# Denominators from sums over 384 of 512 queries, weights one load earlier, norm scratch in the destination, and a new table of shifts

## The chip, the cores and the metric

The kernel runs on one core of a Trainium2 chip. The time of a run is the device time in microseconds (us) of that core, and a kernel's time is the median of its runs. The core has a tensor engine (TensorE, PE in the profile, with its weight loads as PEld), a vector engine (VectorE, DVE), an activation engine (ScalarE, ACT), GpSimd (POOL) and a queue for transfers (SyncE, SP). Each works through its own list of instructions in order and waits for the others through semaphores.

## The reference

An attention layer with a compressive memory and a feed-forward layer, in bf16, over 2048 tokens of width 1024. The 32 heads have width 32; the tokens come in four segments of 512. Cut to what is computed:

```python
def _A_ref(x, wq, wk, wv, wo, beta):          # H = 32, Dh = 32, N = 4 segments, L = 512
    phi = lambda t: where(t > 0, t + 1.0, exp(t))
    g = sigmoid(beta)                          # per head
    M, z = 0, 0
    for s in range(N):
        qs, ks, vs = q[:, :, s], k[:, :, s], v[:, :, s]
        logits = einsum('bhqd,bhkd->bhqk', qs, ks) * Dh ** -0.5 + causal_mask
        a_dot = softmax(logits) @ vs
        pq = phi(qs)
        a_mem = (pq @ M) / (pq @ z + 1e-06)
        outs.append(g * a_mem + (1.0 - g) * a_dot)
        pk = phi(ks)
        M = M + einsum('bhld,bhle->bhde', pk, vs)
        z = z + sum_l(pk)
    return concat(outs) @ wo

def reference(...):
    h = x + _A_ref(layernorm(x), wq, wk, wv, wo, beta)
    n = layernorm(h)
    return h + (silu(n @ w1) * (n @ w3)) @ w2  # w1, w3: 1024 x 3584; w2: 3584 x 1024
```

## The kernel before

**Staging.** The activations of a segment are normalised, transposed (the first segment on TensorE, later ones by a transposing DMA) and projected to q, k and v (`project`), with weights that stream in in halves of 1 MB (`wp`). Then come, for each segment and each half of the heads (16 heads, four groups of four), the attention steps of `attention`; then the output projection and the residual (`wo_stage`, L1361), the second norm (`ln`, L880), and the feed-forward layer in two blocks of 1024 tokens (`ffn_up`, L1389 to L1397, and `ffn_down`). All dense matmuls are recorded at L747 and the transposes of the start at L759; evictions from PSUM are at L770 (ACT) and L771 (DVE).

**Attention of a half.** `scores` (L1081) makes ten sets of scores. A set is four concurrent row tiles of 32 contracted elements (L1101), is followed by one exponential of 2048 columns on ACT into a buffer `et` (L1115), and by a causal mask on GpSimd for the tiles on the diagonal (L1124). Keys are taken in blocks of 128 (`kc` 0 to 3), queries before a key block are left out, so that block `kc` has 512 - 128 kc columns. `finish` (L1159) then makes the numerators (`et` against `v`) and the denominators (`et` against ones) as column tiles, four heads at once (`column`, L1187 and L1194), in four numerator columns with the denominators ahead of the last one. After them ACT and DVE copy the numerators out (`Nsb`, L1245 and L1246), DVE transposes the denominators (`T`, L1225) and takes reciprocals (L1236), and these are spread over the rows by transposes (L1257), or, in the segments 2 and 3, by a trip through a buffer in DRAM, `r_scr` (written by a load-list entry recorded at L322, read back at L1281). The retrieve from the memory is a matmul with 32x32 tiles (L1316), whose result is scaled on DVE (`R`, L1329) and added into `oT` on GpSimd or DVE (L1332); `oT` is what the output projection reads. `attention` calls the retrieve of a half in the middle of the next half's scores.

**Sums for the denominators.** A denominator is a sum over all keys. To spare TensorE a part of it, `gather` (L1131, adds at L1138) adds the exponentials of different key blocks on DVE. Before, for the queries from 256 on, all four key blocks are added: per pair of head groups six adds, four of 4x256 columns and two of 4x128. TensorE then takes per head three pieces: key block 0 for the queries below 256, the sum for those from 256 on, and key block 1 for the queries 128 to 255, which makes 256 + 256 + 128 columns. The two sum buffers of a half lie over `R0` and `R1`, which are not in use then.

**The start.** `first_half` (L961) lists the loads of the first segment: x tiles 0, 1, 2, the first half of the first wq, x tile 3, the first half of the first wk, the rest of them and wv. They go through one queue in this order. `first_tile` (L891) normalises an x tile, transposes it on TensorE in two halves, and evicts the transposes. The statistics of tile 2 wait until the first half of tile 0 has been normalised.

**What sets the order.** The kernel text declares operations with their reads and writes. A planner (`Graph.schedule`) runs a list scheduler over them with a cost for each, and writes a fixed order for every engine; semaphores are then placed from that order. An operation has a class and a sequence number, and the ready operation with the lowest pair goes first. A table `SHIFT` changes both per unit (a unit is about one group of declared operations): the first number moves the sequence, the second the class. Costs in the planner only shape the order. Between the last scores of a half and its column work no transfers are put into the queue.

**Norm scratch.** Some of the second norms (`ON_ACT`) take their statistics on ACT, by two activations whose summed output is what counts; the full-width output is written to a buffer `junk` that nothing reads.

Of the kernel before, what the change touches and what calls it, by code (L numbers as in the profile page):

```python
# [25 lines left out]
ADDED = ((1, 2, 3),) * 4  # L26
# [4 lines left out]
    0: (-18, 0), 3: (-173, 0), 4: (-182, 0), 5: (1074, 0), 6: (1041, 1), 7: (-959, -1),  # L31
    8: (-283, 1), 9: (1560, 1), 10: (-14, 0), 11: (1, 0), 12: (51, -1), 13: (-257, 0),
    14: (-1703, 0), 15: (2952, 0), 16: (-2912, 0), 18: (-87, -1), 19: (3455, 1), 20: (-401, -1),
    21: (22, 0), 22: (2924, -1), 23: (-669, 0), 24: (-328, -1), 26: (-261, -1), 27: (11, -1),
    28: (-153, 0), 29: (-317, 0), 31: (1524, -1), 32: (211, 0), 33: (-1, 0), 34: (2, 0),
    35: (-15, 0), 38: (118, 1), 39: (2057, 0), 40: (223, 0), 41: (2279, -1), 42: (914, 1),
    43: (-1135, 1), 44: (2665, 1), 45: (3218, 1), 47: (1997, 1), 48: (664, -1), 49: (1928, -1),
    50: (-2800, -1), 51: (7, 0), 52: (-1130, 0), 53: (116, 0), 54: (669, 0), 55: (1018, 0),
    56: (2, 0), 57: (-289, 1), 58: (4, 0), 59: (731, 0), 60: (-304, 0), 61: (-436, 0),
    62: (64, 1), 63: (-3, 0), 64: (-63, 0), 65: (-50, 0), 66: (-174, 0), 67: (-937, 0),  # L40
    68: (808, 0), 69: (1512, -1), 70: (28, 0), 71: (-58, 1), 72: (1441, 1), 73: (-75, 1),
    74: (2141, 0), 75: (778, 1), 76: (-752, 1), 77: (90, 1), 78: (-21, 0), 79: (151, 0),
    80: (1343, 0), 81: (-1130, 0), 83: (160, 0), 84: (687, 0), 85: (-676, 0), 86: (312, 0),
    87: (-266, 0), 88: (-263, 0), 89: (-1189, -1), 90: (-164, 0), 91: (680, 1), 92: (-1801, 0),
    93: (1499, 0), 94: (3153, 0), 95: (-261, 0), 96: (0, -1), 97: (-11, 0), 98: (2, 0),
    99: (944, 0), 100: (-54, 0), 101: (1016, 0), 102: (-842, 0), 103: (147, 0), 104: (-1191, 0),
    106: (-47, 0), 107: (121, 1), 108: (-1142, 0), 109: (-1295, -1), 111: (699, 0),
    112: (-365, -1), 113: (-594, 0), 115: (28, 0), 116: (2452, -1), 117: (-8, 0), 118: (676, 0),
    119: (54, 0), 120: (-1449, -1), 121: (235, 0), 122: (-9, -1), 123: (-13, 1), 124: (45, 0),
    125: (-1279, 1), 127: (-283, -1), 129: (555, 0), 130: (1438, -1), 132: (617, 1),  # L50
    133: (81, 0), 134: (-2285, -1), 135: (-179, 0), 136: (3199, 1), 137: (389, 0),
    138: (920, 0), 139: (146, 1), 140: (687, 1), 141: (27, 0), 142: (-619, 1), 143: (1934, 1),
    144: (-922, 0), 145: (415, -1), 146: (-312, 0), 147: (-26, 0), 148: (-870, 0),
    149: (2501, 1), 150: (1682, 0), 151: (-28, 0), 152: (609, 1), 153: (611, 0), 154: (-302, 0),
    156: (0, 1), 157: (-185, 1), 158: (391, 0), 159: (-373, 0), 160: (-610, 0), 161: (-1748, 0),
    162: (-133, 0), 163: (-4056, 1), 164: (1073, 1), 166: (-202, 0), 168: (-3204, -1),
    169: (-2075, -1), 170: (2581, -1), 171: (-39, 1), 172: (-122, 1), 173: (-18, 1),
    174: (-37, 0), 175: (34, 0), 176: (1853, 1), 177: (-140, 0), 178: (-301, 0), 179: (204, 0),
    181: (165, 0), 182: (-13, 0), 183: (-7, 0), 184: (687, -1), 185: (-271, 0), 186: (-861, 1),
    187: (-616, 1), 188: (355, -1), 189: (-1449, 1), 190: (1132, 0), 191: (114, 0),  # L60
    192: (-22, 0), 193: (-464, 0), 194: (-2, 0), 195: (294, 0), 196: (18, 0), 197: (-2089, 0),
    199: (-2443, 0), 200: (248, -1), 201: (1, 0), 203: (210, 1), 204: (-1070, 0), 206: (-70, 0),
    207: (1441, 0), 208: (525, 0), 209: (839, 0), 210: (10, 0), 211: (-262, 0), 212: (894, -1),
    213: (203, 1), 214: (-359, 1), 215: (-2, 0), 216: (696, -1), 217: (-735, 0), 218: (-51, 0),
    219: (4750, 0), 220: (-465, -1), 221: (-23, 0), 222: (-196, 1), 223: (399, 0),
    224: (-1932, 1), 225: (-192, 0), 226: (-134, 0), 227: (-1542, 1), 229: (153, 1),
    230: (-676, 1), 231: (-73, 0), 232: (618, 1), 234: (-465, 0), 235: (0, -1), 237: (222, -1),
    238: (609, 0), 239: (1282, 0), 241: (-183, 1), 242: (845, 1), 243: (811, -1),
    244: (1681, -1), 246: (6, 1), 248: (-2423, -1), 249: (11, 0), 250: (21, 0), 251: (-2902, 1),
    252: (-599, 1), 253: (927, 0), 255: (308, -1), 256: (4, -1), 257: (-382, 0), 258: (30, 0),  # L70
    259: (-35, 0), 260: (-73, -1), 261: (-386, 0), 262: (-58, 1), 263: (-1713, 0),
    264: (-165, 0), 265: (-369, 1), 266: (-12, 0), 267: (808, -1), 268: (1356, 0),
    269: (-538, 0), 270: (576, -1), 272: (27, 0), 273: (609, 0), 275: (-27, 0), 277: (0, -1),
    279: (-4, 0), 280: (-3, 0), 281: (176, 0), 282: (-28, -1), 284: (-175, -1),
    285: (-1255, -1), 286: (-196, 0), 287: (308, 0), 288: (1028, 0), 289: (-18, 0),
    290: (-217, -1), 291: (628, 0), 292: (21, 0), 293: (11, 0), 294: (1042, 0), 295: (6, 0),
    296: (150, -1), 297: (222, 0), 298: (1329, 0), 299: (-799, 0), 300: (-3, 0), 301: (303, -1),
    302: (-473, -1), 303: (2419, -1), 304: (528, 0), 305: (-99, 0), 306: (2531, -1),
    307: (-28, 0), 309: (-1338, 1), 310: (-4, 1), 311: (836, 0), 312: (-154, 0), 315: (-261, 0),
    316: (443, 0), 317: (-31, -1), 318: (-1464, -1), 319: (-220, 0), 320: (340, 0),  # L80
    321: (1268, 0), 322: (-21, -1), 323: (-2755, 1), 324: (-54, 0), 325: (1643, -1),
    326: (-57, 0), 327: (1851, 0), 328: (-2912, 0), 329: (317, 1), 330: (-690, 0),
    331: (-712, -1), 332: (-940, 0), 333: (-1099, 1), 334: (-615, 1), 335: (-16, 0),
    336: (496, 0), 337: (664, 0), 338: (-166, 0), 339: (-46, 0), 340: (-700, 0), 341: (-385, 1),
    342: (-1713, 0), 344: (51, 0), 345: (-756, -1), 346: (178, -1), 348: (803, 0),
    350: (1942, -1), 351: (169, 0), 352: (-492, 1), 354: (14, 0), 355: (-39, 0), 356: (290, 0),
    357: (99, 0), 358: (-389, 0), 359: (1761, 0), 361: (1409, 0), 362: (-58, -1), 363: (550, 1),
    364: (-95, 1), 365: (-140, 1), 366: (56, 1), 367: (-11, 1), 368: (-1627, 0),
# [519 lines left out]
class Kernel:  # L608
# [480 lines left out]
    def scores(self, s, g0, i, parts, at):  # L1089
# [38 lines left out]
        if s == 0 and not g0 and i == GATES:  # L1128
            self.gates()

    def gather(self, i, at, added):  # L1131

        pair, i = divmod(i, 5)
        S, g = self.sums[pair], 2 * pair
# [6 lines left out]
        for n, step in ((0, 1), (1, 4)):  # L1141
            todo = {0: 3 * n, 1: step, 2: 2, 3: step}
            s, done = S[:, :, n, :], None
            for kc in sorted((0,) + added, key=lambda kc: (max(todo[kc], todo[0]), kc != 0, kc == 3)):
                when = max(todo[kc], todo[0])
                if when > i:
                    break
# [363 lines left out]
```

The softmax here doesn't subtract the row's maximum and nothing guards it: scores larger than these inputs give would overflow.

## Time and profile before

| | before |
|---|---|
| time, median of 3 runs | 888.77 us (888.38 to 888.92) |
| span of the profiled run | 886.3 us, TensorE clock 1.000 |
| TensorE busy | 873.0 us, 99% of the span |
| VectorE busy | 449.2 us, 51% |
| ScalarE busy | 302.5 us, 34% |
| GpSimd busy | 178.4 us, 20% |

A line of a group of instructions reads: line of the kernel, engine, operation, output and inputs by name with their shape, number; then busy time in us and the mean of one in ns; then the idle time of the engine just before such instructions and what ended it. A line of the timeline begins with the start and the length in us, and a bracket at its end tells how long the engine was idle before and what ended that. Matmuls overlap, so the mean of one is longer than the distance between two. "ps" is PSUM.

### The profile page before, as it was taken

The page shows a single profiled execution, that of the slowest core. Times are in us where ns is not written, and L with a number is a line of the kernel's source. Part 1 is how long each engine was busy: PE and PEld are TensorE (multiplying, and loading weights), DVE is VectorE, ACT ScalarE, POOL GpSimd, SP SyncE. Part 2 cuts the span into 40 slices and gives each one's busy share as a digit, 9 for nine tenths or more (in the row PEclk, how much of TensorE's full clock was granted, in tenths as well). Part 3 has the DMA queues.
Part 4 walks back from the last instruction along what each step waited for, and adds up shares of the span by engine and source line. Part 5 has one row for each costly group of instructions (what it writes and reads, how often), then busy time and mean ns, then how long its engine had stood idle before and what let it go on. Part 6 is the DMA issues. An engine that isn't in the chain of part 4 may idle for free.

```text
span 886.3 us, 13649 instructions
## 1 busy us (share of the span) xinstructions
PE 873.0 (99%) x5732; PEld 400.5 (45%) x5821; DVE 449.2 (51%) x699; ACT 302.5 (34%) x345; POOL 178.4 (20%) x226
## 2 busy tenths in 40 slices
PE   9999999999999999999999999999999999999998
PEld 5444444444444344444444444444444444444445
DVE  6697878786665797645545301323243333341011
ACT  5878675779645555511111000101011111110000
POOL 2544443455252455303000000000000000000000
PEclk9999999999999999999999999999999999999999
DMA  7869939464862736198354410221323321301010
GB/s 238 208 185 244 227 91 267 125 156 119 217 155 74 175 83 156 53 300 258 103 156 107 120 35 30 78 65 54 83 61 88 95 72 48 90 7 41 30 54 24
DMA packets 148796, 105.75 MB, mean 119 GB/s; under 512 B 46336, under 2 KB 134400, under 8 KB 147712
## 3 DMA queue, kind: packets, MB, share of 16 engines
q1 hardware_dynamic: 148736, 104.89, 44.5%
q8 instruction: 46, 0.75, 0.4%
q14 instruction: 14, 0.11, 0.0%
HBM read 84.94 MB, written 9.44 MB: 106 GB/s over the span
## 4 chain that ended last, share of the span: by engine, by line
PE 94%; DMA 2%; DVE 2%; issue 1%; POOL 0%; ACT 0%; SPq 0%; ACTq 0%; POOLq 0%; DVEq 0%
PE ps L747 88%; PE ps L1194 3%; PE ps L1101 3%; DMA R0w<-r_scr 1%; DMA r_scr<-T 1%; DVE oT L1332 0%; SPq L1281 0%; DMA xs<-in_A_x_dram 0%; PE ps L1029 0%; DVE lnst L874 0%; ACT et L1115 0%; PE ps L1316 0%; POOL et L1124 0%; DVE hm L1397 0%; PE ps L1187 0%
## 5 line engine op out<-in xcount | busy, mean ns | idle before, releaser
L747 PE MATMUL ps<-hnT,w1b 128*128 128x512 bf16 x875 | 219.8, 379 | 2.0 <-issue 0.5
L747 PE MATMUL ps<-hnT,w3b 128*128 128x512 bf16 x879 | 217.1, 379 | 1.5 <-issue 0.5
L747 PE MATMUL ps<-w2b,hm 128*128 128x512 bf16 (+2 forms) x935 | 198.5, 366 | 0.9
L1389 ACT ACTIVATE sg<-ps 128x512 bf16<-128x512 f32 x112 | 66.8, 597 | 385.9 <-PE ps L747 385.8
L1392 DVE SCALAR_TENSOR_TENSOR t<-sg,ps 128x512 bf16<-128x512 bf16 x112 | 76.7, 685 | 183.1 <-ACT sg L1389 182.6
L1115 ACT ACTIVATE et<-ps 128x2048 bf16<-128x2048 f32 x80 | 150.0, 1874 | 45.1 <-PE ps L1101 44.7
L747 PEld LDWEIGHTS ps<-w2b,hm 128*128 128x128 bf16 x952 | 90.9, 98 | 103.0
L747 PEld LDWEIGHTS ps<-hnT,w1b 128*128 128x128 bf16 x896 | 86.2, 98 | 106.3 <-issue 6.5
L747 PEld LDWEIGHTS ps<-hnT,w3b 128*128 128x128 bf16 x896 | 86.3, 98 | 106.1 <-issue 3.6
L1124 POOL TENSOR_SCALAR_AFFINE_SELECT et<-et 128x512 bf16<-128x512 bf16 (+1 forms) x96 | 93.1, 976 | 133.0 <-ACT et L1115 132.7
L1397 DVE SCALAR_TENSOR_TENSOR hm<-t,ps 128x512 bf16<-128x512 bf16 x112 | 76.2, 685 | 40.8 <-PE ps L747 39.0
L1421 DVE TENSOR_TENSOR ob<-hr,ps 128x512 bf16<-128x512 bf16 (+2 forms) x34 | 22.2, 655 | 120.6 <-PE ps L747 120.4
L747 PE MATMUL ps<-wo,oT 128*128 128x512 bf16 x246 | 60.9, 379 | 1.1 <-issue 0.8
L747 PE MATMUL ps<-xnT,wp 128*128 128x512 bf16 (+1 forms) x345 | 59.6, 320 | 1.3 <-issue 0.8
L747 PE MATMUL ps<-hnT,wp 128*128 128x512 bf16 x249 | 59.4, 380 | 0.8 <-issue 0.6
L1138 DVE TENSOR_TENSOR sum<-sum,et 128x512 bf16<-128x512 bf16 (+1 forms) x64 | 43.6, 684 | 11.6 <-POOL et L1124 6.1
L747 PEld LDWEIGHTS ps<-xnT,wp 128*128 128x128 bf16 x352 | 28.0, 98 | 26.9 <-issue 2.8
L747 PEld LDWEIGHTS ps<-wo,oT 128*128 128x128 bf16 x256 | 23.9, 98 | 29.9 <-issue 3.3
L747 PEld LDWEIGHTS ps<-hnT,wp 128*128 128x128 bf16 x256 | 23.5, 98 | 29.7 <-issue 3.9
L1101 PE MATMUL ps<-qT,kT 32*128 32x128 bf16 (+3 forms) x512 | 31.7, 301 | 0.0
L747 PE MATMUL ps<-wp,xnT 128*128 128x512 bf16 x123 | 30.2, 379 | 0.4 <-issue 0.2
L747 PE MATMUL ps<-wp,hnT 128*128 128x512 bf16 x123 | 29.6, 380 | 0.5 <-issue 0.3
(97 smaller groups left out, 560.1 us busy)
## 6 DMA issues: line engine op xcount, KB each, us to landing
w3b<-in_B_w_dram SPq DMA_DIRECT2D x28, 512.0 KB, 4.1
w1b<-in_B_w_dram SPq DMA_DIRECT2D x28, 512.0 KB, 4.0
wp<-in_A_wv_dram SPq DMA_DIRECT2D x8, 1024.0 KB, 6.5
wp<-in_A_wq_dram SPq DMA_DIRECT2D x7, 1024.0 KB, 5.6
wp<-in_A_wk_dram SPq DMA_DIRECT2D x7, 1024.0 KB, 7.2
w2b<-in_B_w_dram SPq DMA_DIRECT2D x7, 1024.0 KB, 5.8
xs<-in_A_x_dram SPq DMA_DIRECT2D x16, 256.0 KB, 5.9
h<-in_A_x_dram SPq DMA_DIRECT2D x16, 256.0 KB, 4.0
```

The costliest lines, as they stand in the source:

```text
L747: return [e.matmul(p[0](gr), p[1], p[2], start=p[3], stop=p[4]) for p in part]
L1101: ins.append(e.matmul(self.bank(gr, j, 512 - 128 * kc, off), k[r, g0 + g, 128 * kc:128 * kc + 128], q[r, g0 + g, 128 * kc:512], start=True ...
L1115: return [e.activation(et[:, :, :], src, AF.Exp, scale=self.scale)]
L1124: self.pool_op(lambda e, v=v, pat=pat: e.affine_select(v, v, pattern=pat, compare_op=ALU.is_ge, fill=0.0, base=0, channel_multiplier=-1), ...
L1138: lambda e, gr: [e.tensor_tensor(out, x, y, op=ALU.add)], reads=[x, y],
L1194: ins.append(e.matmul(self.ps[32 * i:32 * i + 32, b * 512 + c0:b * 512 + c0 + n], lhsT(i, kc, j), rhs(i, j), start=kc == 0 and j == first, ...
L1389: self.g.op("act", act_ns(512), lambda e, gr, sg=sg: [e.activation(sg, self.bank(gr), AF.Tanh, scale=0.5)], writes=[sg], cls=0, group=gg)
L1392: e.scalar_tensor_tensor(t1, sg, 1.0, self.bank(gr), op0=ALU.add, op1=ALU.mult)], reads=[sg], writes=[t1], cls=0,
L1397: e.scalar_tensor_tensor(dst, t1, 0.5, self.bank(gr), op0=ALU.mult, op1=ALU.mult)], reads=[t1], writes=[dst], cls=0,
L1421: self.g.op("dve", dve_ns(n), lambda e, gr, hs=hs, ob=ob, n=n: [e.tensor_tensor(ob, hs, self.bank(gr, 0, n), op=ALU.add)], reads=[hs], wri ...
```

## The change

Five edits are made together.

1. The sums take in all queries but the first 128 (384 columns instead of 256). TensorE needs two pieces per head instead of three: key block 0 for the first 128 queries, and the sum for the other 384. `gather` makes seven adds per pair instead of six: for the first head group of a pair 4x384, 4x128 and 4x256 columns, for the second 4x256, 4x256, 4x128 and 4x128. This is to take work off TensorE.
2. The two sum buffers become 6144 bytes each and lie one after the other over `R0`, 2048 free bytes and the beginning of `R1`. The bytes come from `junk`: the norm's activations write their unused output into `hn`, where the normalised row is put afterwards.
3. The first half of the first wq is loaded ahead of x tile 2, so that the first projection can begin earlier.
4. The first eviction of tile 0's transposes is put on VectorE, and the statistics of tile 2 wait for it.
5. The table `SHIFT` is another one throughout, so the order on every engine changes, in the feed-forward layer less than in the attention.

The diff without the table and without the lines of the removed name `ADDED`:

```diff
-        self.junk = buf("junk", [128, 1024], BF16)
...
         self.R0 = buf("R0", [128, 2, 512], F32)
+        take(2048)
         self.R1 = buf("R1", [128, 4, 512], F32)
...
-        self.sums = [buf(f"sum{i}", [128, 4, 2, 256], BF16, self.g.base[t.name][1])
-                     for i, t in enumerate((self.R0, self.R1))]
+        self.sums = [buf(f"sum{i}", [128, 4, 2, 384], BF16, self.g.base[self.R0.name][1] + 6144 * i)
+                     for i in range(2)]
...
-        var, mean, op = self.ln_act(k, src, self.junk[:, :], cls - 1) if k in ON_ACT else self.ln_stats(k, src, cls - 1)
+        var, mean, op = self.ln_act(k, src, dst, cls - 1) if k in ON_ACT else self.ln_stats(k, src, cls - 1)
...
-            t, x, 1, (self.applied[0],) if t else ())
+            t, x, 1, (self.copied,) if t else ())
...
-            self.evac(gr, out, 512, lambda v: v[:, 0:512].rearrange("p (k n) -> p k n", k=4),
-                      cls=1, bf=True, engs=("dve", "act"))
+            o = self.evac(gr, out, 512, lambda v: v[:, 0:512].rearrange("p (k n) -> p k n", k=4),
+                          cls=1, bf=True, engs=("dve", "act") if t or b else ("dve",))
+            if t == 0 and not b:
+                self.copied = o
...
-        loads = [x[0] + (1.04,), x[1] + (0.7,), x[2] + (1.2,),
-                 (wq[:, :, 0:256], sq[:, :, 0:256], 1.54), x[3] + (0.65,),
+        loads = [x[0] + (1.04,), x[1] + (0.7,), (wq[:, :, 0:256], sq[:, :, 0:256], 1.3),
+                 x[2] + (1.0,), x[3] + (0.65,),
...
-        for n, step in ((0, 1), (1, 4)):
-            todo = {0: 3 * n, 1: step, 2: 2, 3: step}
-            s, done = S[:, :, n, :], None
-            for kc in sorted((0,) + added, key=lambda kc: (max(todo[kc], todo[0]), kc != 0, kc == 3)):
-                when = max(todo[kc], todo[0])
-                if when > i:
-                    break
-                x = at[g + n, kc][:, :, 256 - 128 * kc if kc < 2 else 0:512 - 128 * kc]
-                if done is None:
-                    done = x
-                    continue
-                if when == i:
-                    if kc == 3:
-                        add(s[:, :, 128:256], s[:, :, 128:256], x, 512)
-                    else:
-                        add(s, done, x, 1024)
-                done = s
+        for n in range(2):
+            D, s = S[:, :, n, :], [at.get((g + n, kc)) for kc in range(4)]
+            if n == 0 and i == 1:
+                add(D, s[0][:, :, 128:512], s[1], 1536)
+                add(D[:, :, 256:384], D[:, :, 256:384], s[3], 512)
+            elif n == 0 and i == 2:
+                add(D[:, :, 128:384], D[:, :, 128:384], s[2], 1024)
+            elif n == 1 and i == 3:
+                add(D[:, :, 128:384], s[0][:, :, 256:512], s[2], 1024)
+            elif n == 1 and i == 4:
+                add(D[:, :, 128:384], D[:, :, 128:384], s[1][:, :, 128:384], 1024)
+                add(D[:, :, 256:384], D[:, :, 256:384], s[3], 512)
+                add(D[:, :, 0:128], s[0][:, :, 128:256], s[1][:, :, 0:128], 512)
...
-        denom = [(0, lambda i, j: at[i, 0][:, j, 0:256], 0, 256),
-                 (1, lambda i, j: self.sums[i // 2][:, j, i % 2, :], 256, 256)] if added else numer[:1]
-        for kc in (1, 2, 3):
-            n = (128 if kc == 1 else 0) if kc in added else 512 - 128 * kc
-            if n:
-                denom.append((kc, lambda i, j, kc=kc, n=n: at[i, kc][:, j, 0:n], 128 * kc, n))
+        denom = [(0, lambda i, j: at[i, 0][:, j, 0:128], 0, 128),
+                 (1, lambda i, j: self.sums[i // 2][:, j, i % 2, :], 128, 384)]
```

The table's first entries, as an example of what it holds:

```diff
-    0: (-18, 0), 3: (-173, 0), 4: (-182, 0), 5: (1074, 0), 6: (1041, 1), 7: (-959, -1),
+    0: (2251, 0), 3: (-192, 0), 4: (703, 0), 5: (938, 0), 6: (37, 0), 7: (-2876, -1),
```

## The prediction

> **What bounds the kernel now.** I read the engine totals first, then the chain that ended last, then the groups of instructions by shape, and last the timeline around the places that the change touches.
>
> ```profile
> PE 873.0 (99%) x5732; PEld 400.5 (45%) x5821; DVE 449.2 (51%) x699; ACT 302.5 (34%) x345; POOL 178.4 (20%) x226
> PE 94%; DMA 2%; DVE 2%; issue 1%; POOL 0%; ACT 0%; SPq 0%; ACTq 0%; POOLq 0%; DVEq 0%
> ```
>
> TensorE (PE) is busy all the time and is 94% of the chain. So a microsecond of TensorE work removed is worth a microsecond, work of another engine costs nothing while TensorE has something to do, and every new hole in TensorE's stream is paid in full. From start to start of consecutive matmuls (a dense 128x512 one every 0.216 us) I find only 3.7 us of real holes in 886.3: 1.22 in the first 12 us, and 2.45 later, at 174.5 (0.33), 257.7 (0.13), 266 (0.38), 297.8 (0.92), 308.7 (0.54) and 457.5 (0.15).
>
> ```profile
> L1115 ACT ACTIVATE et<-ps 128x2048 bf16<-128x2048 f32 x80 | 150.0, 1874 | 45.1 <-PE ps L1101 44.7
> L1124 POOL TENSOR_SCALAR_AFFINE_SELECT et<-et 128x1024 bf16<-128x1024 bf16 x32 | 45.3, 1417 | 60.1 <-ACT et L1115 60.1
> L1138 DVE TENSOR_TENSOR sum<-sum,et 128x1024 bf16<-128x1024 bf16 x32 | 29.8, 933 | 9.5 <-ACT et L1115 5.3 <-POOL et L1124 4.2
> L1138 DVE TENSOR_TENSOR sum<-et,et 128x1024 bf16<-128x1024 bf16 x32 | 26.7, 838 | 4.4 <-ACT et L1115 4.4
> L1332 POOL TENSOR_TENSOR oT<-Nsb,R 128x512 bf16<-128x512 f32 x15 | 22.4, 1515 | 1.4 <-DVE R L1329 1.4
> L1138 DVE TENSOR_TENSOR sum<-sum,et 128x512 bf16<-128x512 bf16 x32 | 13.9, 435 | 2.1 <-POOL et L1124 2.0
> L1194 PE MATMUL ps<-et,ones 128*32 128x256 bf16 x128 | 8.9, 273 | 0.0
> L1194 PE MATMUL ps<-sum,ones 128*32 128x256 bf16 x128 | 8.9, 273 | 0.0
> L1194 PE MATMUL ps<-et,ones 128*32 128x128 bf16 x128 | 7.4, 219 | 0.0
> ```
>
> The price list: an exponential 1.87 us, the mask of a last tile 1.42, one product into oT 1.52, an add 0.44 to 0.93. The last three rows are the denominators; their means are latencies of overlapped matmuls, so I price them from starts:
>
> ```profile
> 93.44 0.28 PE L1194 MATMUL ps<-et,ones 128*32 128x256 bf16 x4
> 93.55 0.28 PE L1194 MATMUL ps<-sum,ones 128*32 128x256 bf16 x4
> 93.66 0.34 PE L1194 MATMUL ps<-et,ones 128*32 128x128 bf16 x8
> ...
> 94.48 0.23 PE L1194 MATMUL ps<-et,ones 128*32 128x128 bf16 x4
> 94.53 0.72 PE L1194 MATMUL ps<-et,v 128*32 128x512 bf16 x16
> ```
>
> One round of 256+256+128 columns takes 0.273 us; four rounds make the 1.09 us from 93.44 to 94.53. Now two chains that decide how long TensorE must have other work. From the last scores of a half to its numerators:
>
> ```profile
> 170.93 0.40 PE L1101 MATMUL ps<-qT,kT 32*128 32x128 bf16 x8
> 171.44 1.88 ACT L1115 ACTIVATE et<-ps 128x2048 bf16<-128x2048 f32 x1 [1.06 <-PE ps L1101]
> ...
> 173.38 1.62 POOL L1124 TENSOR_SCALAR_AFFINE_SELECT et<-et 128x1024 bf16<-128x1024 bf16 x1 [2.29 <-ACT et L1115]
> ...
> 175.14 1.81 PE L1194 MATMUL ps<-et,v 128*32 128x512 bf16 x48 [0.26 <-POOL et L1124]
> ```
>
> Scores end, exponential, mask, numerators: with 1.87, the mask's 1.42 to 1.62 and about 0.4 of handing over, 3.7 to 4.0 us. Here 3.65 us of TensorE work lay between, and 0.33 us was stalled. From a retrieve to the output projection that reads its product:
>
> ```profile
> 193.19 0.43 PE L1316 MATMUL ps<-pq,Mbf 32*32 32x512 bf16 x16
> ...
> 194.58 1.63 POOL L1332 TENSOR_TENSOR oT<-Nsb,R 128x512 bf16<-128x512 f32 x1 [0.52 <-DVE R L1329]
> ...
> 198.99 2.94 POOL L1332 TENSOR_TENSOR oT<-Nsb,R 128x512 bf16<-128x512 f32 x2
> ```
>
> The fourth oT is there 8.7 us after the retrieve began; with no gap on GpSimd (POOL) it would be 1.39 + 4 x 1.515 = 7.5. The first projection came at 203.92 and lost nothing.
>
> **What the Trainium skill says.** "TensorEngine Tiling (Array Packing)", Key Properties: a change of tiling mode drains TensorE. The trace agrees: between 84.35 and 87.05 lie 12 dense matmuls (2.59) and a change to row tiles, so about 0.10 us. "SBUF — State Buffer", Summary: VectorE (DVE) with two SBUF inputs and GpSimd reading SBUF lock each other out. It fits the mask above, 1.62 us beside adds from 173.35 on, against a mean of 1.42. "DMA: Bandwidth & Descriptors", Anatomy of one DMA: 2 us plus bytes at 436 GB/s, which would be an estimated 4.4 us for 1 MB; the trace is slower, medians of 5.6 (wq) and 7.2 us (wk), 5.1 at best. The measured ones are used.
>
> **The change, part by part.**
> *Denominators.* 128+384 columns instead of 256+256+128: 0.273 x 512/640 = 0.218 us a round, 0.219 less per half, eight halves: -1.75 us. 128 fewer matmuls.
> *Adds.* Per pair of head groups seven adds instead of six and 1024 more elements, 16 pairs: from (838 - 435)/512, 0.79 ns an element, plus the extra instruction (435 - 403 = 32 ns), 16 x 0.84 = 13.5 us more of VectorE. It is 51% busy, but 70 to 80% in the attention part, so most of it hides beside TensorE. They lie ahead of evictions in VectorE's queue, and lock out GpSimd's masks; bounds 0 and 1.5 us, I take 0 here and let the stalls below carry it.
> *Memory and norm output.* Writing into hn instead of a scratch buffer, and the moved sums, add no instruction; that work is on ACT, 34% busy: 0.
> *Mode changes.* In the built order TensorE changes mode 191 times instead of 188; two column stages are cut by dense work. 3 x 0.10 to 0.15: +0.35.
> *Start.* The profile of before:
>
> ```profile
> 7.79 0.83 PE L747 MATMUL ps<-xnT,wp 128*128 128x128 bf16 x12 [0.31 <-ACT xnT L770]
> ...
> 11.01 2.40 PE L747 MATMUL ps<-xnT,wp 128*128 128x128 bf16 x40
> ```
>
> The first wk half landed at 10.46 and was first used at 11.01. It is still the sixth load, so it lands then again. In the new order only 16 transposes and 16 quarter-width wq matmuls (about 1.8 us) stand between the first tile's eviction and the first wk matmul. They are done by about 9.2, so TensorE waits some 1.25 us there. The first eviction on VectorE (0.41) rather than ACT (0.60) gives 0.2 back. Bounds +0.3 and +1.5: I take +1.0.
> *Shifts.* They decide how much TensorE work lies between a chain's cause and its user. I counted that in the built order, by the measured pitch, for every wait of TensorE. Where it is below what the chains above need, the difference is a stall. Positions are TensorE work from the start, real time being 5 to 7 us later:
> - 161, numerators of the second half of segment 1: 8 dense matmuls (1.8 to 1.9 us) after the last scores against 3.7 to 4.0: +1.9.
> - 185, projection of segment 1: 5.7 to 5.9 us after the retrieve with four products on GpSimd, 7.5 to 8.7 needed: bounds +1.6 and +2.9, less what it shares with the scores behind it: +1.8.
> - 126 and 145, scores 1.93 us after scores, where hand-over and one exponential need 2.2 (before's smallest was 2.37), with 1 MB of wk asked for 5.2 and 5.6 us before its use: bounds +0.5 and +2.5, I take +1.0.
> - 265, an up projection 0.86 us after its gate, where tanh (0.60), product (0.69) and hand-over need over 1.5, and a retrieve behind it: +0.8.
> - the retrieves at 222 and 308, 18.5 and 18.0 us after their numerators, where before needed 18.4 to 19 (it stalled 0.92 at 297.8 for this reload): bounds 0 and +2.8, I take +0.5.
> That is +6.0, and the 2.45 us of before's later holes are gone with its order.
> Sum: -1.75 + 0.35 + 1.0 + 6.0 - 2.45 = +3.15, so 888.8 + 3.2 = 892.0 us.
>
> **Rivals.**
> (a) The waits are all absorbed, because chains run faster than I priced or slip with an earlier stall; the denominators remain: 888.8 - 1.75 + 0.35 = 887.4, or 885 if before's 2.45 us are gained as well. For it: TensorE's work itself shrinks. Against it: a mask cannot start before its exponential, so the 161 hole alone takes back 1.9.
> (b) Half: start +0.3, later stalls 3.7: 888.8 - 1.4 + 0.3 + 3.7 - 2.45 = 889.0. For it: a stall lets the other engines catch up, so neighbouring ones don't add.
> (c) More: the r_scr reloads at their upper bound (+2.3), the adds' lock-out (+1.5): 895.8. For it: the 0.92 us stall on such a reload before.
>
> **How the numbers follow.** The forecast (890.6 to 895) has 0.60, (a) 0.12, (b) 0.18, (c) 0.10. The likeliest gives 892.0. The range takes (b) and a part of (a) and the lower part of (c): 887.4 to 895.0. Within 0.2% is 887.0 to 890.5: (b) and part of (a), 0.21. Faster: the rest of (a) 0.10. Slower: 0.69.
>
> **What would show it.** Denominator rounds of 0.22 us; wk's first matmul waiting for its DMA with TensorE idle around 9.3 to 10.5; a hole of nearly 2 us before column matmuls near 167, ended by GpSimd's mask; one before the projection near 191, ended by GpSimd's oT; VectorE about 13 us busier, with the span unmoved by it. I am wrong if the second and third hole are missing, which would mean that my count of the work between is wrong, or if holes appear in the feed-forward half, where I count none.

## The result, and the profile after

The changed kernel takes 895.46 us (median of 4 runs, 893.1 to 896.76) against 888.58 in the same session: ratio 1.0076, 95% interval 1.0053 to 1.0098. It is slower, as forecast, but by 6.9 us and not by 3.2, and 0.5 us above the top of the range. The profiled spans are 893.4 and 886.3 us, so the profile has 7.1 us to explain.

The engine totals and the shares of the chain, from the page of the changed kernel:

```profile
PE 878.7 (98%) x5693; PEld 396.8 (44%) x5693; DVE 455.6 (51%) x712; ACT 302.7 (34%) x345; POOL 181.9 (20%) x229
PE 90%; DMA 6%; POOL 1%; ACT 1%; DVE 1%; SPq 0%; issue 0%; ACTq 0%
```

TensorE is still nearly always busy, but its share of the chain (the run of waits and work that ended last) fell from 94 to 90%, and transfers went from 2 to 6%. Something now waits for loads. The changed groups by shape (busy time, mean ns of one, idle time ahead and its cause):

```profile
L1106 ACT ACTIVATE et<-ps 128x2048 bf16<-128x2048 f32 x80 | 150.0, 1875 | 34.9 <-PE ps L1092 34.2
...
L1129 DVE TENSOR_TENSOR sum<-et,et 128x1536 bf16<-128x1536 bf16 x16 | 15.6, 973 | 4.8 <-POOL et L1115 4.8
...
L1129 DVE TENSOR_TENSOR sum<-et,et 128x512 bf16<-128x512 bf16 x16 | 8.6, 538 | 5.0 <-POOL et L1115 5.0
L1176 PE MATMUL ps<-sum,ones 128*32 128x384 bf16 x128 | 8.0, 326 | 0.0
...
L849 ACT ACTIVATE hn<-h 128x1024 bf16<-128x1024 bf16 x6 | 6.3, 1051 | 0.0
```

The exponentials cost what they did. The first add of a pair (128x1536) waits for GpSimd's mask; before, the first add of a pair waited for exponentials alone. The norm passes into `hn` wait for nothing.

Now the second half of segment 1, where the prediction put its largest hole; TensorE's timeline (start, duration of the group):

```profile
170.88 0.40 PE L1092 MATMUL ps<-qT,kT 32*128 32x128 bf16 x8
171.22 1.90 PE L736 MATMUL ps<-hnT,wp 128*128 128x512 bf16 x8
175.04 1.81 PE L1176 MATMUL ps<-et,v 128*32 128x512 bf16 x48 [1.93 <-POOL et L1115]
...
176.88 0.24 PE L1176 MATMUL ps<-et,ones 128*32 128x128 bf16 x4
176.94 0.35 PE L1176 MATMUL ps<-sum,ones 128*32 128x384 bf16 x4
177.10 0.24 PE L1176 MATMUL ps<-et,ones 128*32 128x128 bf16 x4
```

Two readings. Eight matmuls end and the numerators wait 1.93 us for the mask. And a round of denominators takes 177.10 - 176.88 = 0.22 us, down from 0.273.

From start to start I sum the holes of both traces (the last two columns in us):

| place (us in the trace after) | what ended it | counted in the prediction | measured |
|---|---|---|---|
| start, 7 to 14 | wk load 1.03, VectorE and ACT 0.93 | +1.0 over before | 1.96 against 1.01, so +0.95 |
| first transposes | x tile 0; at 6.98 instead of 6.63 | none | +0.35 |
| 135.9, 136.5, 156.0 | exponential 0.21, wk load 0.34 and 0.78 | 1.0 | 1.33 |
| 172.7 | mask | 1.9 | 2.00 |
| 198.6 | fourth `oT` on GpSimd | 1.8 | 1.24 |
| 280.6, 282.2 | gate 0.80, `r_scr` 0.57 | 0.8 | 1.37 |
| retrieves at 237.4 and 325.9 | | 0.5 | 0 |
| 21.8, 27.1 | exponential 1.00, eviction of `qT` on ACT 0.18 | none | 1.18 |
| 32.5 | wq load | none | 1.37 |
| 128.5, 352.0 | mask, 0.27 each | none | 0.54 |
| 566.0, 777.1 | loads of the feed-forward half | none | 0.70 |
| before's later holes | | -2.45 | -2.45 |
| denominators with mode changes | | -1.40 | -1.34 |

Before's 1.01 are holes of 0.48, 0.25 and 0.28 between its first transposes and 14 us; the 1.22 that the prediction gives for its start is 0.2 more. The places counted, from 135.9 on, give 5.94 against 6.0; those not counted, from 21.8 on, 3.79 against 0. The sum is 0.95 + 0.35 + 5.94 + 3.79 - 2.45 - 1.34 = +7.2, against 7.1 us between the spans. (In four of the eight halves a round of the phase sits next to dense work, and the phase takes 0.98 to 0.99 instead of 0.87 us; the 1.34 contains that.)

The largest holes not counted. First the one near 22, all engines:

```profile
18.87 0.69 DVE L863 BATCH_NORM_STATS2 lnst<-xs 128x6 f32<-128x512 bf16 x1 [3.00 <-DMA xs<-in_A_x_dram]
...
19.48 0.67 DVE L760 CAST kT<-ps 128x512 bf16<-128x512 f32 x1
...
20.25 1.06 ACT L711 ACTIVATE phe<-kT 128x1024 bf16<-128x1024 bf16 x1 [1.98 <-DVE kT L760]
...
21.21 1.86 ACT L1106 ACTIVATE et<-ps 128x2048 bf16<-128x2048 f32 x1
...
23.13 0.40 PE L1092 MATMUL ps<-qT,kT 32*128 32x128 bf16 x8 [0.93 <-ACT et L1106]
```

Read it upwards. The second scores wait for the first exponential. That stands in ACT's queue behind `phe`, which waits for VectorE's eviction of `kT`. ACT evicts the other half at 17.00, but in VectorE's queue the eviction stands behind statistics of an x tile (in `e4` below, where nothing stands ahead of it, it begins at 17.60), and VectorE idles 3.00 us for that tile's load. One late 256 KB load goes through three in-order queues into TensorE. In before's trace the same tile was there at 17.93, and no scores waited.

Then the one near 32, with the transfer that ended it, from the list of DMA issues between 15 and 37 us (last number: us from issue to landing):

```profile
32.39 0.40 PE L1092 MATMUL ps<-qT,kT 32*128 32x128 bf16 x8
34.09 1.25 PE L736 MATMUL ps<-xnT,wp 128*128 128x512 bf16 x5 [1.30 <-DMA wp<-in_A_wq_dram]
```

```profile
wp<-in_A_wq_dram SPq DMA_DIRECT2D x1, 1024.0 KB, 7.8
wp<-in_A_wk_dram SPq DMA_DIRECT2D x1, 1024.0 KB, 6.1
```

The load was asked for 6.4 us ahead of its user; I had priced it at the median of 5.6.

### The profile page after: what moved, and what is told of

It is laid out like the page before. It is cut to its first block, busy times and chain, and to the rows that moved or that the text cites. A ratio compares the mean times of both kernels' runs of the same rounds, so it can differ in the third digit from the quotient of the medians.

```text
span 893.4 us, 13458 instructions
## 1 busy us (share of the span) xinstructions
PE 878.7 (98%) x5693; PEld 396.8 (44%) x5693; DVE 455.6 (51%) x712; ACT 302.7 (34%) x345; POOL 181.9 (20%) x229
## 4 chain that ended last, share of the span: by engine, by line
PE 90%; DMA 6%; POOL 1%; ACT 1%; DVE 1%; SPq 0%; issue 0%; ACTq 0%
PE ps L736 84%; PE ps L1176 3%; PE ps L1092 3%; DMA xs<-in_A_x_dram 2%; DMA wp<-in_A_wk_dram 1%; DMA wp<-in_A_wq_dram 1%; ACT et L1106 1%; DMA R<-r_scr 1%; POOL oT L1314 1%; DMA r_scr<-T 1%; POOL et L1115 1%; DMA w3b<-in_B_w_dram 0%; DMA hr<-h_scr 0%; PE ps L1020 0%; PE ps L1298 0%
## 5 line engine op out<-in xcount | busy, mean ns | idle before, releaser
L1115 POOL TENSOR_SCALAR_AFFINE_SELECT et<-et 128x512 bf16<-128x512 bf16 x96 | 89.8, 941 | 105.3 <-ACT et L1106 105.3
L736 PE MATMUL ps<-xnT,wp 128*128 128x512 bf16 (+1 forms) x352 | 61.6, 321 | 2.3 <-DMA wp<-in_A_wq_dram 1.3
L1129 DVE TENSOR_TENSOR sum<-et,et 128x1536 bf16<-128x1536 bf16 (+2 forms) x48 | 38.0, 793 | 12.9 <-POOL et L1115 9.8
L873 POOL TENSOR_SCALAR lnve<-lnmv 128x1 f32<-128x1 f32 x22 | 6.4, 292 | 123.3 <-DVE lnmv L866 123.3
```

Of the source, the lines that this page charges most:

```text
L736: return [e.matmul(p[0](gr), p[1], p[2], start=p[3], stop=p[4]) for p in part]
L873: self.g.op("pool", 240.0, lambda e, gr: [e.tensor_scalar(ve, var, self.EPS, None, op0=ALU.add)], reads=[var], writes=[ve], cls=0)
L1115: self.pool_op(lambda e, v=v, pat=pat: e.affine_select(v, v, pattern=pat, compare_op=ALU.is_ge, fill=0.0, base=0, channel_multiplier=-1), ...
L1129: lambda e, gr: [e.tensor_tensor(out, x, y, op=ALU.add)], reads=[x, y],
```

## The experiments

Except for the changed kernel itself, most kernels here keep the order that one table gives and replace single instructions in it, so that one part changes at a time. The edits are shown in short form. `e1`, `e2`, `e5`, `e6`, `e9` and `e10` have the 384 columns of a sum in the room of the 256-column ones, where two head groups share 256 columns, so their sums are not the right ones; `e13` at the end gives them room of their own. Medians of the kernel before in the same sessions were 888.75 to 889.12 us.

### Which part costs what

**e1**, before's order, with the changed denominators and adds:

```diff
-        denom = [(0, lambda i, j: at[i, 0][:, j, 0:256], 0, 256),
-                 (1, lambda i, j: self.sums[i // 2][:, j, i % 2, :], 256, 256)]
+        denom = [(0, lambda i, j: at[i, 0][:, j, 0:128], 0, 128),
+                 (1, lambda i, j: self.wide(i // 2, i % 2)[:, j, :], 128, 384)]
...
-                        add(s, done, x, 1024)
+                add(D, s[0][:, :, 128:512], s[1], 1536)
...
```

The new first add of a pair takes in key block 1 for the queries 128 to 255, which the mask treats; before, its columns needed no mask.

> The kernel before with its own order of work on every engine, in which only the denominators change: 128 + 384 columns on TensorE instead of 256 + 256 + 128, and the adds of the changed kernel (seven instructions for six, the two extra 128-column adds of a pair given out together). The wide sums lie over each other in the small buffers of before, so their values are not the reference's; their sizes and waits are those of the changed kernel. Theory (the new table of shifts makes the holes, the denominators save what was counted): 888.6 - 1.75 = 886.8 us, denominator rounds of 0.22 us, VectorE 13 us busier. Rival 1 (the bigger adds and their wait for GpSimd's masks hold up VectorE and through it TensorE): 890 us or more, with new holes ended by VectorE or GpSimd.

889.38 us, ratio 1.0006 (0.9997 to 1.0015): no gain. The denominator phases did shrink, from 8.77 to 6.99 us in the eight halves, so 1.8 us was won and given back.

**e5**, the adds alone, and **e6**, the pieces on TensorE alone:

```diff
# e5: the adds
-                        add(s, done, x, 1024)
+                add(D, s[0][:, :, 128:512], s[1], 1536)
...
# e6: the pieces
-        denom = [(0, lambda i, j: at[i, 0][:, j, 0:256], 0, 256),
+        denom = [(0, lambda i, j: at[i, 0][:, j, 0:128], 0, 128),
...
```

> The kernel before in its own order, with the denominators of before on TensorE but the changed kernel's adds on VectorE (seven for six, 1024 more elements a pair, and the wait of the first for GpSimd's mask); the sums lie over each other, so their values are not the reference's. It asks where the 1.79 us that e1 took off TensorE went. Theory A (the adds stand ahead of evictions in VectorE's queue and give the gain back): 889.1 + 1.5 to 2 = 890.6 to 891.1 us, with holes of over 0.5 us ended by VectorE near 272 and 363. Theory B (the gain is lost to loads that land as late as before, whatever TensorE does): 889.1 us, no new hole ended by VectorE.

> The other half of e1: the kernel before in its own order, with 128 + 384 columns of denominators on TensorE and the adds of before; the 384 columns are read from where sums lie, with values that are not the reference's. Theory A (adds): 889.1 - 1.8 = 887.3 us. Theory B (loads): 889 us, with holes ended by DMA in the place of the 1.8 us.

e5: 889.63 us, ratio 1.0014 (1.0008 to 1.0021), by the ratio +1.25 us (0.7 to 1.9). e6: 887.17 us, 0.9984 (0.9978 to 0.9991), by the ratio -1.4 us. So the gain is real, and the adds give it back. e1 and e5 both have holes of 0.76 us near 272 and 0.56 near 363; e6 has neither.

**e2**, e1 and the edit of the start (first weights ahead of the third x tile, first eviction on VectorE):

```diff
-loads: x0, x1, x2, wq first half, x3, wk first half
+loads: x0, x1, wq first half, x2, x3, wk first half
```

> As e1, and also the start of the changed kernel: the first wq half ahead of x tile 2 in the queue, the first eviction on VectorE, the statistics of tile 2 behind it; still the order of before on TensorE. That is the whole change but for the table (and the norm scratch). Theory: the start costs 0 to 0.8 us, so 886.8 to 887.6 us. Rival 2 (the start makes most of the loss): 890 us or more.

890.57 us, 1.0016 (1.0008 to 1.0025), 1.2 us over e1. Its start has holes of 0.59, 1.26 and 0.77 us, 2.6 in all against 1.0 before. They are not the whole loss: after them, from 9.76 to 13.17 us, the granted clock of TensorE was 0.50, and matmuls of 128 columns came every 0.107 us instead of 0.056, which makes some 1.3 us more. Seven of the 22 executions have a mean clock of 0.998, like this one, and a median of 891.2 us; the other 15, at 1.000, one of 889.9, 0.5 over e1. No execution of the changed kernel shows this. So e2 does not measure the +1.0 that I gave the start.

**e3**, the changed order with the denominators, adds and load order of before (the first eviction stays on VectorE):

```diff
-SHIFT = {0: (-18, 0), 3: (-173, 0), 4: (-182, 0), 5: (1074, 0), 6: (1041, 1),
+SHIFT = {0: (2251, 0), 3: (-192, 0), 4: (703, 0), 5: (938, 0), 6: (37, 0),
...
```

> The order of work of the changed kernel, with the denominators and adds of before (three pieces, six adds) and x tile 2 ahead of wq again: the new table by itself. Theory: the changed kernel's 895.5 + 1.75 for the denominators - 0.3 for the loads = 897 us, with the changed kernel's holes at the same places. Rival 1 and 2 (denominators or start cost the time): 889 to 891 us, near the kernel before.

899.2 us, 1.0116 (1.0103 to 1.0129): +10.1 us. The table alone is worse than the whole change. The hole ahead of the numerators is there at the same size (1.92 us idle), those of the projection (1.24) and near 21 (1.21) as well, and the reload of `r_scr` (1.15) and the residual (0.86) lost more in this execution. The parts are not additive: e2 against before gives +1.4 by its ratio, and 1.0116 for the table would make about 901.

### Two holes taken away

**e4**, the changed kernel with `kT`'s eviction ahead of the statistics of the x tile, the four `R` of the retrieve in a row on VectorE, and the fourth `oT` on VectorE:

```diff
-dve:  statistics(x tile), kT, ...        R0, sum, R1, pq, R2, pq, R3
-pool: oT0, oT1, oT2, oT3
+dve:  kT, statistics(x tile), ...        R0, R1, R2, R3, oT3, sum, pq, pq
+pool: oT0, oT1, oT2
```

> The changed kernel, with two repairs in the written order: VectorE evicts the key group (kT) before the statistics of the next segment's x tile instead of behind them; and at the retrieve near 193 us VectorE scales its four parts in a row and makes the fourth product into oT itself. Theory: the hole of 1.0 us near 22 (ended by the first exponential) and that of 1.24 us near 199 (ended by GpSimd's oT) go: 895.5 - 2.2 = 893.3 us. Rival 3 (the holes belong to longer chains and come back behind the place): 895 us, with new holes within 20 us behind each.

894.78 us, 1.0062 (1.005 to 1.0074), not clear of the changed kernel's 1.0053 to 1.0098. The x tile came as late as before (statistics at 18.93), but the hole near 22 fell from 1.00 to 0.45 us and is now ended by `qT`: the place of the eviction behind the statistics made the difference. The one ahead of the projection is gone, but the next scores now wait:

```profile
198.30 1.04 PE L809 MATMUL ps<-wo,oT 128*128 128x512 bf16 x4
200.35 0.40 PE L1165 MATMUL ps<-qT,kT 32*128 32x512 bf16 x4 [1.01 <-ACT et L1179]
```

In the changed kernel the wait for `oT` had hidden the wait for the exponential (1.88 us from 198.97 there). With one gone the other shows: only 4 dense matmuls stand between two sets of scores at this place. The order is short of TensorE work here, and taking away one wait uncovers the next.

### The start and the late load

**e7**, the changed kernel with the third x tile ahead of wq again; **e8**, the changed kernel with the transposing transfer held back until wq has landed:

```diff
# e7
-loads: x0, x1, wq first half, x2
+loads: x0, x1, x2, wq first half
# e8
+    g.dep(hnT_transpose, wq_load)
```

> The changed kernel with x tile 2 ahead of the first wq half in the queue again, all else as changed. Theory (the load moved does not help, since the first projection waits for x tile 0's normalising and the wk half is the sixth load in both): x tile 0 lands near 3.6 instead of 4.0, the first projection starts near 7.6 instead of 7.97, the wait for wk near 9.7 stays at 1.0 to 1.3 us, total 895.5 - 0.3 = 895.2 us. Rival (the earlier wq is worth something): 896 us or more.

> The changed kernel, in which the transposing DMA of a row of the next segment (issued near 27.5 us) waits until the wq half issued near 26.3 has landed. Theory (the transposing DMA takes the engines that the load needs): the load lands 5.4 us after its issue instead of 7.8, near 31.7, and the hole of 1.37 us near 32.5 goes; the rows come later, which may cost elsewhere, so 894 to 895.5 us. Rival (this load takes 7 to 8 us by itself): it lands near 34 and the hole stays.

e7: 894.85 us, 1.0071 (1.0057 to 1.0085); e8: 895.29 us, 1.0083 (1.0065 to 1.01). Both intervals overlap the 1.0053 to 1.0098 of the changed kernel. In e8's trace the wq load landed 5.5 us after its issue and the hole near 32 is gone, as the theory of the transposes in its way wants:

```profile
wp<-in_A_wq_dram SPq DMA_DIRECT2D x1, 1024.0 KB, 5.5
```

But in e7 it landed after 6.0 and in e3 after 5.4 us, with the transposing transfer in flight. All traces together: with no transpose issued within 4 us behind it (e8 and the nine in before's order) the load took 5.1 to 5.5 us; with one issued 1.2 to 1.4 us behind it, 7.6 to 7.9 in the three with wq ahead of the third x tile (changed kernel, e4, e12) and 5.4 and 6.0 in the two with the x tile first (e3, e7). So a transpose close behind goes with every late landing but is not enough for one; whether the order of the loads or chance decides the rest, five traces can't tell.

The medians of e7 and e8 hardly gain from the hole that is gone. Their traces have 1.36 and 1.26 us at a load of `w3b` near 621, and e12's has 1.36, where the changed kernel's and e4's have none.

### What ate the denominators' gain

The theory after e5: a product of the feed-forward layer (`hm` or `t`), which TensorE waits for, stands in VectorE's queue behind the first wide add, and that add now waits for the mask. The same stretch of before and of e1, all engines:

```profile
268.38 0.69 DVE L1138 TENSOR_TENSOR sum<-et,et 128x1024 bf16<-128x1024 bf16 x1 [0.62 <-ACT et L1115]
268.42 1.61 POOL L1124 TENSOR_SCALAR_AFFINE_SELECT et<-et 128x1024 bf16<-128x1024 bf16 x1 [3.07 <-ACT et L1115]
...
269.44 0.69 DVE L1397 SCALAR_TENSOR_TENSOR hm<-t,ps 128x512 bf16<-128x512 bf16 x1 [0.37 <-PE ps L747]
```

```profile
269.94 1.10 POOL L1194 TENSOR_SCALAR_AFFINE_SELECT et<-et 128x1024 bf16<-128x1024 bf16 x1 [3.07 <-ACT et L1185]
...
271.14 0.96 DVE L1229 TENSOR_TENSOR sum<-et,et 128x1536 bf16<-128x1536 bf16 x1 [1.86 <-POOL et L1194]
...
272.01 0.68 DVE L1494 SCALAR_TENSOR_TENSOR hm<-t,ps 128x512 bf16<-128x512 bf16 x1
...
272.75 0.60 PE L817 MATMUL ps<-hnT,w3b 128*128 128x512 bf16 x2 [0.60 <-DVE hm L1494]
```

Before, the add starts with the mask. In e1 it starts after it, takes 0.96 us, and `hm` follows; TensorE stands still for `hm`.

**e9**, e1 with four such products moved ahead of the add; **e10**, e1 with the add split, so that the masked 128 columns are added by themselves behind the mask:

```diff
# e9
-dve: sum 1536, hm
+dve: hm, sum 1536
# e10
-add(D, s[0][:, :, 128:512], s[1], 1536)
+add(D[:, :, 128:384], s[0][:, :, 256:512], s[1][:, :, 128:384], 1024)
...
+add(D[:, :, 0:128], s[0][:, :, 128:256], s[1][:, :, 0:128], 512)
```

The last line stands at the end of a pair's first group, as it already does in the second.

> As e1 (the order of before, denominators and adds of the changed kernel, sums lying over each other so that their values are not the reference's), with one difference in VectorE's order: where the first, wide add of a pair stood directly ahead of a feed-forward product (four places, two of them the holes near 272 and 363), the product goes first. Theory A (that add waits for GpSimd's mask with the product queued behind it): the holes of 0.76 and 0.56 us go, e1's ratio of 1.0006 falls by 1.3 us to 0.9991, 888 us where before takes 888.8. Rival (VectorE simply has too much to do): the ratio stays at 1.0006.

> As e1, but the first add of a pair leaves out the 128 masked columns, as the adds of before did, and takes them in an instruction of their own behind the mask, with key block 3: eight adds a pair, none of the first waiting for GpSimd (values as in e1). Theory A: the adds' cost goes with the wait although VectorE does more, so the ratio is near e6's 0.9984, 887.4 us where before takes 888.8. Rival (length and number of adds): 889.5 us or more.

e9: 886.88 us, 0.9983 (0.9973 to 0.9992). e10: 887.72 us, 0.9989 (0.9981 to 0.9996), with more VectorE work than e1. In both the holes near 272 and 362 are gone. The list of waits (total us, times, longest) for e1 and for e10:

```profile
DVE sum L1229 <- POOL et L1194: 15.4, 13, 2.4
```

```profile
DVE sum L1228 <- POOL et L1194: 4.5, 7, 1.1
```

Before it was 6.1 us, with 1.1 the longest. (e9 has 8.5, with 1.6 the longest.) It is the wait at the head of the queue, with a product behind it, that costs; the amount of adding does not.

**e12**, the changed kernel with the split add:

```diff
-add(D, s[0][:, :, 128:512], s[1], 1536)
+add(D[:, :, 128:384], s[0][:, :, 256:512], s[1][:, :, 128:384], 1024)
...
+add(D[:, :, 0:128], s[0][:, :, 128:256], s[1][:, :, 0:128], 512)
```

> The changed kernel with its adds split as in e10, everything else as it was. Theory (its loss is in the places counted from its order, which the adds don't end): 895.5 - 0.0 to 0.5 = 895 to 895.5 us where before takes 888.8, the ratio 1.0070 to 1.0076. Rival (the adds' wait for the mask makes part of the loss there too): 894 us or less.

895.28 us, 1.0069 (1.0056 to 1.0082): no different from the changed kernel. In its order none of the listed holes is ended by a product behind an add, so there was nothing to win.

### A version that beats both

**e11**, the split add and room for the sums, with before's order up to 422 us and the feed-forward work after that planned anew; **e13**, the same with before's order throughout, where the six norm passes write into places that are idle at that time:

```diff
-self.sums = [buf(f"sum{i}", [128, 4, 2, 256], BF16, ...
+self.wide = [buf(f"wide{i}", [128, 4, 2, 384], BF16, ...
...
-self.ln_act(k, src, self.junk, cls - 1)
+self.ln_act(k, src, self.scratch[k], cls - 1)
```

> The version that the runs point to, with the reference's values: the order of before up to 427 us, denominators of 128 + 384 columns, adds split as in e10, the wide sums in room of their own, and the scratch of the norm passes in places that are idle at the time. In the feed-forward layer the order is planned anew, because the buffers lie elsewhere. Theory A: as e10, 887.4 us where before takes 888.8. Rival: the feed-forward layer's new order or the scratch costs the 1.4 us, 888.8 us or more.

> The order of work of the kernel before on TensorE throughout, the changed kernel's denominators (128 + 384 columns), the wide add split so that the 128 masked columns are added by themselves behind the mask, every query counted. The wide sums have room of their own: six normalization passes write into places that are idle at that time, so no order has to change in the feed-forward half. Theory (an add that waits for the mask with a product behind it was all that ate the denominators' gain): 888.9 x 0.9989 = 887.9, ratio 0.998 to 0.9995, no hole over 0.5 us near 272, 362 or 422. Rival 1 (the gain of the kernels without all queries came from data or sums that are wrong in value): ratio 1.000 or above. Rival 2 (the loss of the earlier version with its own sums was the extra VectorE work in the attention half, not the new feed-forward order): 1.002 to 1.003 again.

e11: 891.47 us, 1.0026 (1.0018 to 1.0034). Nine of its 13 executions have the mean clock of 0.998 that e2 showed; the traced one does not. Its trace has one new hole, 2.47 us from start to start, where the part that was planned anew begins:

```profile
421.16 1.03 PE L834 MATMUL ps<-hnT,w1b 128*128 128x512 bf16 x4
...
424.49 0.81 PE L834 MATMUL ps<-hnT,w1b 128*128 128x512 bf16 x3 [2.30 <-DVE hm L1514]
```

In the order of before, three products (12 matmuls) stand between these two groups and hide the chain from gate to `hm`. The same place in e13:

```profile
420.68 1.03 PE L837 MATMUL ps<-hnT,w1b 128*128 128x512 bf16 x4
421.54 2.75 PE L837 MATMUL ps<-hnT,w3b 128*128 128x512 bf16 x12
424.13 1.03 PE L837 MATMUL ps<-hnT,w1b 128*128 128x512 bf16 x3
```

e13 tells whether that hole or the adds were to blame: 887.3 us (22 runs) against 888.75, ratio 0.9987 (0.998 to 0.9993). It is faster than before and than the changed kernel, and its sums are the right ones, so the gain of e6, e9 and e10 does not come from their shared room. The stretch near 270 in its trace, all engines:

```profile
268.85 0.69 DVE L1252 TENSOR_TENSOR wide<-et,et 128x1024 bf16<-128x1024 bf16 x1 [0.62 <-ACT et L1213]
268.88 1.62 POOL L1222 TENSOR_SCALAR_AFFINE_SELECT et<-et 128x1024 bf16<-128x1024 bf16 x1 [3.07 <-ACT et L1213]
...
269.90 0.69 DVE L1517 SCALAR_TENSOR_TENSOR hm<-t,ps 128x512 bf16<-128x512 bf16 x1 [0.36 <-PE ps L837]
...
270.60 0.42 DVE L1252 TENSOR_TENSOR wide<-wide,et 128x512 bf16<-128x512 bf16 x1
...
270.99 0.42 DVE L1252 TENSOR_TENSOR wide<-et,et 128x512 bf16<-128x512 bf16 x1
```

The first add runs beside the mask again, `hm` follows in its old place, and the two small adds that need the mask come after it. And VectorE's total on its page:

```profile
PE 871.3 (98%) x5604; PEld 396.6 (45%) x5693; DVE 462.0 (52%) x731; ACT 302.6 (34%) x345; POOL 179.2 (20%) x226
```

VectorE works 12.8 us longer than before, and the kernel is 1.2 to 1.5 us faster.

## Why the prediction was right or wrong

*Right: the direction and its reason.* The change trades 1.4 us of TensorE work for an order with too little work between causes and users. e3 shows that the table alone costs 10.1 us, e2 that all the rest but the norm output costs 1.4 in before's order, e6 that the denominators alone gain 1.4.

*Right: denominators.* Rounds of 0.22 us, net -1.34 against -1.40.

*Right in size: the start.* +0.95 against +1.0, with the wk load ending a hole of 1.03 us that opens at 9.7, as forecast. The 0.35 us by which the first transposes came later were not forecast; over all traces they came between 6.43 and 6.98, in both orders of the loads, so I don't put this down to the change.

*Right: the places that were counted.* 5.94 against 6.0, but the close sum is partly luck, for the parts differ: the reload of `r_scr` lost 0.57 us behind the gate at 280.6 and nothing at the retrieves at 237.4 and 325.9, and the projection lost 1.24 instead of 1.8, below its bound of 1.6. There the `R` came 1.3 to 1.4 us apart, faster than the products took them, so GpSimd ran its four without a gap, 5.69 us, and the fourth was there 7.1 us after the retrieve began, not 7.5 to 8.7.

*Wrong: the step "I counted that in the built order ... for every wait of TensorE".* The list it gave was not complete, and in the trace the missing places cost 3.79 us, which is the miss. They are of these kinds:
- Chains that begin with a load and not with TensorE (1.00). The hole near 22 starts with an x tile that landed at 18.85, and e4 halved it by moving one eviction. I measured only the TensorE work between a TensorE cause and its user.
- Loads at a single price (1.37). The wq load near 32 had 6.4 us and I allowed 5.6; it took 7.8 there, 7.9 in e4, 7.6 in e12, 6.0 in e7.
- Numerators behind a mask at 128.5 and 352.0 (0.54), and a short wait at 27.1 (0.18). These repeat in e3 and e4 within 0.01 us where they are ended by the mask, and could have been counted.
- The feed-forward half, "where I count none": 0.70 us at two loads. The prediction named this as a way to be wrong.

This list is an account of one trace. Taking single holes away (e4, e7, e8) moved the median by 0.2 to 0.7 us, not clear of noise, because others opened. And the first two kinds are not the new order's alone. In e1, e5, e9 and e11, which have before's order at this place, the x tile's statistics started at 18.97 to 19.20 and holes of 0.96 to 1.19 us came near 21; in before's own profile they started at 17.93 and there was none. Waits for a wq load, 0.65 to 1.58 us each, stand in the traces of e1, e2, e9, e10, e11 and e13 too, near 77, 103 and 197; before's own has none. So a comparison of two profiles puts more on the change than is its own there. Before's profiled run was 0.6 us below its median, the changed kernel's 0.4, so little of the 6.9 us is luck of this kind.

*Wrong: the adds at 0.* My bounds were 0 and 1.5; e5 measures 1.25 in before's order. I saw that the adds lie ahead of evictions in VectorE's queue, but argued from VectorE's share of busy time and priced them by the element. The price was one add whose input comes later than before (the mask), with a product behind it: e9 and e10 remove that and keep the elements. In the changed order no hole of this kind is among those listed, and e12 gains nothing from splitting, so this error did not make the miss of the forecast. The adds took 81.3 us after and 70.4 before, +10.9 against my +13.5 (VectorE's total rose by 6.4). My price per element came from means that contain waits behind masks: an add of 1024 columns takes 0.68 us when GpSimd does nothing, against means of 0.84 and 0.93.

*Still open.* Why e3 is 3.7 us slower than the changed kernel. Its trace, 3.3 us longer, has 1.79 us more of denominators (9.22 against 7.44), a hole of 1.09 near 133 ended by VectorE's copy of the numerators, 0.58 and 0.49 more at `r_scr` and the residual and 1.2 in four short holes between 184 and 318; against that it lacks the 1.37 near 32 and 0.8 of the start. What opens the four short ones is not shown. Open is also what, besides a transpose close behind, makes the same load take 5.4 us in one execution and 7.9 in another.

## What to carry to other kernels

When one engine sets the time, list every wait of that engine back through all in-order queues to its first cause, the transfers included, and give each load its slow landing time and not its median. A sum that is cheap on an idle engine is not free if one of its inputs comes later than before: look at what stands behind it in that queue, and split off the part that needs the late input. A hand-shaped order belongs to the set of operations it was shaped for; try the new operations in the old order first.

## What the runs showed of the hardware

- The same 1 MB load of wq, asked for near 25 us, landed 5.4 (e3), 5.5 (e8), 6.0 (e7), 7.6 (e12), 7.8 (changed kernel) and 7.9 us (e4) after its issue. The Trainium skill, "DMA: Bandwidth & Descriptors", Anatomy of one DMA, has the fit behind the estimate of 4.4 us that the prediction quotes; the page heads it with the path of transfers issued by GpSimd, and these are issued by SyncE. The fastest 1 MB of wq or wk in any trace here took 5.0 us (e5, issued at 158.4).
- The x tile whose statistics VectorE waits for near 18 us let them start anywhere from 17.79 (e7) to 19.20 us (e11), in both orders. In before's order the hole near 21 was 0 with a start by 18.22 (before, e6, e13), 0.27 at 18.36 (e10) and 0.96 to 1.19 from 18.97 on (e1, e5, e9, e11); e2, where TensorE was itself late, had none at 19.07.
- The hole ahead of the numerators of segment 1, whose chain begins with TensorE's own scores, repeats almost exactly: 1.99 to 2.00 us in the changed kernel, e3, e4, e7, e8 and e12. The one near 22, also ended by an engine but with a load in its chain, does not: it was 0.42 (e7), 0.55 (e12), 0.73 (e8), 1.00 (changed kernel) and 1.21 us (e3).
- After holes of 1.26 and 0.77 us at its start, e2's TensorE had a granted clock of 0.50 for 3.41 us. The changed kernel's hole of 2.00 us at 172.7 has nothing of the kind behind it, so these runs give no length from which on a hole costs clock.
- GpSimd's mask of 1024 columns took 1.10 us while VectorE idled for it (e1, 269.94) and 1.61 when it started 0.04 us behind an add of VectorE, which kept its 0.69 (before, 268.38). The other way round the add grows: started 0.05 us behind such a mask (before, 89.66) it took 1.59, and the mask kept its 1.10. The Trainium skill, "SBUF — State Buffer", Summary, says that the second of such a pair is blocked until the first is finished. The traces agree, but for about 0.15 us by which the two overlap.
